# Attention with routed experts: row scaling moves from ScalarE to VectorE, narrowing and first weight splits move behind the second exponential

## The chip, the cores and the metric

The kernel runs on one NeuronCore of a Trainium2 chip. The metric is the device time of one execution in microseconds; the median of several runs counts. The engines are TensorE (PE, with its weight loads as PEld), VectorE (DVE), ScalarE (ACT), GpSimd (POOL) and SyncE (SP), which issues most of the transfers. Each engine works through its own instructions strictly in the order in which the program gives them, and waits on semaphores for the others.

## The reference

```
scores = q k^T / sqrt(D) + bias(|i - j|)         # B=2, H=8, S=576, D=64; bias by a small MLP
attn   = exp(scores - max) / (sum + 1e-9);  x = attn v        # x: N=1152 tokens x 512
expert = argmax(x w_gate); gate = softmax(x w_gate)[expert]   # E=8, at most 288 rows for one expert
moe[i] = gate[i] * relu(x[i] w1[expert]) w2[expert]           # 0 for rows over the capacity
h = moe w_in;  out = (h * cos(h)) w_out                       # 512 -> 2048 -> 512
```

A row can be multiplied by its gate before the two expert matmuls, since relu and matmuls are linear in a positive factor. This product of one tile of rows with its column of gates is the "row's scaling" of the change.

## The kernel before

The attention is cut into 36 steps (`ns`): each is one tile of 128 query rows (`BLOCKS`) and one pair of heads. `step_of(n)` is a software pipeline written out by hand: it emits, for several steps at once, what each engine is to do, and the order of emission is the order on each engine. In step n stand:

- the second exponential of step n, `emit_exp(n, 1)` (line 398, with the sum of the row read out behind it);
- the scores of step n+1 (`emit_qk`, line 381, the banks `sb` for the first head and `sa` for the second), and on VectorE the sums of score and bias with their minimum (`emit_sum`, line 389);
- the transposes of the exponentials of step n in three groups (`emit_tr`, line 412) and their copies on ScalarE (`emit_tev`, line 419, into `et`);
- in steps up to 25, the bias of later tiles: `bias_h` (line 313, four products on VectorE) and `bias_half` (line 337, matmuls into the one bank `bb`, read out on ScalarE by line 338 twice a step, so that the second half waits for the read-out of the first);
- the first exponential of step n+1, then the product with v of step n-1 (`emit_pv`, line 433, into a part of `sa`) and its copy (`emit_xs`, line 443). The next scores for `sa` wait for that copy.

When a tile of rows is complete, `finish_block` puts four small functions on a list that `run_late` works off, one or two a step: `f1` and `f2` (gate logits, line 511 on, the largest and its index; then the marks `nm`, `idxf` and `oh`, lines 523 to 526, on the engine `aux[0]`, which is GpSimd), `f3` (an exponential of 8 columns on ScalarE, line 535) and `f4` (the gate `gt`, lines 541 and 542 on VectorE, and the row's scaling, line 551 on ScalarE, which is put on the list `put_off` and emitted behind the third copy of the step). `route` (line 560) numbers the rows within their experts by matmuls with `oh` and `srun`, works out the destination of each row (`ov`, `wv`, `sl`, lines 586 to 598, on GpSimd) and scatters the rows to DRAM (line 602). For the last tile alone, behind the 36 steps, `aux[0]` is VectorE.

In steps 28 to 32 (`EARLY`) five pieces of `w_in` are narrowed to float32, each by four operations: `mag` (line 709, ScalarE), `shift`, `low` and `sign` (lines 712, 715 and 718, VectorE). `mag` stands in step n-1 ahead of `emit_xs`, that is between the two exponentials of step n. In steps 32 and 33 the first two pieces of the first expert's `w1` are split into a high and a low part (`split1`, line 908 on ScalarE, line 909 on VectorE), at the step's end, also ahead of the second exponential of the next step. In step 35 the rows of the first expert are transposed (`turned`, lines 935 to 937), and from there on the two large experts, a small one and the second layer follow, with TensorE busy nearly throughout.

Of the kernel before, what the change touches and what calls it, by code (L numbers as in the profile page):

```python
# [14 lines left out]
AF = mybir.ActivationFunctionType  # L15
ALU = mybir.AluOpType
# [7 lines left out]
DM = H * D  # L24
# [78 lines left out]
def attention_moe_kernel(  # L103
# [38 lines left out]
    eid, w_tiles = [], {}  # L142
# [350 lines left out]
    def finish_block(b, ib):  # L493
        t = tile_of(b, ib)
        loc = {}

        xs, row, rz = xs_t[b, ib], xn_t[b, ib], rz_t[b, ib]

        def f1():
            ps = late_f1()  # L500
            for p in range(NP):
                T.matmul(out=ps[32 * p:32 * p + 32, :], lhsT=wgs[:, p, :], rhs=xs[:, p, :], start=True, stop=True)
            yield
            A.activation(out=lt_buf[:, :], in_=ps[:, :], func=AF.Copy)

        def f2():
            ps = late_ps()
            T.transpose(ps, lt_buf[:, :], ident)
            yield
            lp = sm_p.tile([128, H, E], F32, tag="lp", bufs=1, name="lp")  # L510
            V.tensor_tensor(
                out=lp.rearrange("p (q u) e -> p q u e", u=2),
                in0=ps.rearrange("p (q z e) -> p q z e", q=NP, e=E)[:, :, 0:2],
                in1=rz.rearrange("p (q u) -> p q u", u=2)[:, :, :, None].to_broadcast([128, NP, 2, E]), op=ALU.mult,
            )
            lg = sm_p.tile([128, E], F32, tag="lg", name="lg")
            V.tensor_reduce(out=lg, in_=lp.rearrange("p h e -> p e h"), axis=AX.X, op=ALU.add)
            top = sm_p.tile([128, 8], F32, tag="top", bufs=2, name="top")
            V.max(out=top, in_=lg)  # L519
            ix = sm_p.tile([128, 8], U32, tag="ix", bufs=2, name="ix")  # L520
            V.max_index(out=ix, in_max=top, in_values=lg)
            nm = sm_p.tile([128, 1], F32, tag="nm", bufs=2, name="nm")
            aux[0].tensor_scalar(out=nm, in0=top[:, 0:1], scalar1=-1.0, scalar2=None, op0=ALU.mult)  # L523
            for t_, a, e in parts_of(b, t):
                aux[0].tensor_copy(idxf[a:e, t_:t_ + 1], ix[a:e, 0:1])
                aux[0].tensor_scalar(
                    out=oh[a:e, t_, :], in0=eio[a:e, 0:E], scalar1=idxf[a:e, t_:t_ + 1], scalar2=None, op0=ALU.is_equal,
                )
            loc.update(lg=lg, nm=nm)

        def f3():
            lg, nm = loc["lg"], loc["nm"]
            ex = sm_p.tile([128, E], F32, tag="ex", bufs=2, name="ex")
            es = sm_p.tile([128, 1], F32, tag="es", bufs=2, name="es")
            A.activation(out=ex, in_=lg, func=AF.Exp, bias=nm, scale=1.0, accum_out=es)
            loc["es"] = es

        def f4():
            es = loc["es"]
            gt = sm_p.tile([128, 1], F32, tag="gt", bufs=2, name="gt")  # L540
            V.tensor_scalar(out=gt, in0=es, scalar1=1e-9, scalar2=None, op0=ALU.add)
            V.reciprocal(out=gt, in_=gt)
            P.memset(row[:, DM:RW], 0.0)
            word = row[:, DM:DM + 1].bitcast(I32)
            P.iota(word, pattern=[[0, 1]], base=128 * ib if b == BOTH else b * S + 128 * ib, channel_multiplier=1)
            if b == BOTH:
                P.tensor_scalar(out=word[64:128], in0=word[64:128], scalar1=S - 64, scalar2=None, op0=ALU.add)
            if aux[0] is V:
                V.tensor_scalar(out=row[:, 0:DM], in0=row[:, 0:DM], scalar1=gt[:, 0:1], scalar2=None, op0=ALU.mult)
            else:  # L550
                put_off.append(lambda: A.activation(out=row[:, 0:DM], in_=row[:, 0:DM], func=AF.Copy, scale=gt[:, 0:1]))
            for t_, a, e in parts_of(b, t):
                row_t[t_] = row

        late.extend([(1, f1), (1, f2)] + [(0, f3)] + [(1, choose)] * ((b, ib) == CHOOSE) + [(0, f4)])
# [4 lines left out]
    def route(ts):  # L560

        def f():
            psr = late_ps()
            for i, t in enumerate(ts):
                before = [srun] + [oh[:, u, :] for u in ts[:i]]
                for j, (w, x) in enumerate([(tri, oh[:, t, :])] + [(ones, x) for x in before]):
                    T.matmul(out=psr[:, E * i:E * i + E], lhsT=w, rhs=x, start=(j == 0), stop=(j == len(before)))
            yield
            for t in ts:
                aux[0].tensor_tensor(out=srun, in0=srun, in1=oh[:, t, :], op=ALU.add)  # L570
            eng = V if len(ts) > 1 and aux[0] is V else P
# [80 lines left out]
    def first_full():  # L652
# [9 lines left out]
        V.tensor_copy(kgi, kg[0:1])  # L662
        V.tensor_scalar(out=other0, in0=gidx, scalar1=float(-E), scalar2=None, op0=ALU.add)

    def run_late(n):
        rest_ = []
        for _ in range(n):
            while late and late[0][0] <= 0:
                whole(late.pop(0)[1])
            if late:  # L670
                g = late.pop(0)[1]()
                if g:
                    next(g)
                    rest_.append(g)
        return rest_

    def go_on(rest_):
        while put_off:
            put_off.pop(0)()
        for g in rest_:  # L680
            next(g, None)

# [125 lines left out]
    def step_of(n):  # L808

        g, nxt = RUNS.get(n), RUNS.get(n + 1)  # L810
        more = None
        if n == TWICE:
            more, nxt = nxt, g + 1
        if n > 1:
            b, ib, p = steps[n - 2]
            if p == NP - 1 and n < SOONER:
                finish_block(b, ib)
                ready.append((b, ib))

        while ready and n >= ROUTE_FROM:  # L820
            tile_done(*ready.pop(0))
        if n > 0:
            emit_exp(n, 1)
        if n + 1 < ns:
            b, ib, p = steps[n + 1]
            j = BLOCKS.index((b, ib))
            for u in range(2):
                emit_qk(n + 1, u)
            if p == 0 and 0 < j < len(BLOCKS) - 1:
                fetch_q(*BLOCKS[j + 1])  # L830
            if n == 0:
                bias_h(g, on_act=ON_ACT)
        hook(n, "start")
        emit_tr(n, 0)
        hook(n, "turned")
        emit_tev(n, 0)
        if n >= LATE_FROM:
            go_on(run_late(LATE_A.get(n, 0)))
        emit_tr(n, 1)
        if n > 1:  # L840
            emit_nat(n - 2)
        emit_tev(n, 1)
        emit_tr(n, 2)
        begun = run_late(LATE_B.get(n, n < LATE_FROM))
        emit_tev(n, 2)
        while put_off:
            put_off.pop(0)()
        if nxt is not None:
            bias_h(nxt, on_act=ON_ACT if n < ACT_TO else (), quads=(0, 1))
        if n in EARLY:  # L850
            for _ in range(2):
                early_ops.pop(0)()
        go_on(begun)
        if g is not None:
            bias_half(g, 0)
        if n > 1:
            emit_nrm(n - 2)
        if n + 1 < ns:
            emit_exp(n + 1, 0)
        if nxt is not None:  # L860
            bias_h(nxt, on_act=ON_ACT if n < ACT_TO else (), quads=(2, 3))
        if n in EARLY:
            early_ops.pop(0)()
        if n + 1 in EARLY:
            early_ops.pop(0)()
        hook(n, "values")
        if 0 < n:
            emit_rz(n - 1)
            emit_pv(n - 1)
            emit_xs(n - 1)  # L870
        if n == SOONER:
            b, ib, p = steps[n - 1]
            finish_block(b, ib)
            tile_done(b, ib)
        go_on(run_late(LATE_C.get(n, 0)))
        if g is not None:
            bias_half(g, 1)
            if more is not None:
                bias_h(more, on_act=ON_ACT)
                bias_half(nxt, 0)  # L880
                bias_half(nxt, 1)
            if g == NG - 1:
                own.append(bb)
        load_step(n)
        if n in FILL_AT:
            i = FILL_AT.index(n)
            fill_rows(256 * i, min(256, E1 * CAP - 256 * i))
            if n == FILL_AT[-1]:
                fill_ids()
        if 17 <= n < 26:  # L890
            fill_out(n - 17)
        hook(n, "end")
# [81 lines left out]
    def expert_end(s, off):  # L974
# [13 lines left out]
        (28, "end"): [lambda: fetch_piece(3), lambda: fetch_w1(eid[0], (1,))],  # L988
        (29, "end"): [lambda: fetch_w1(eid[0], (2,))],
        (30, "end"): [lambda: fetch_w1(eid[0], (3,))],  # L990
        (32, "end"): [lambda: fetch_w2(eid[0], (1,)), lambda: split1(0)],
        (33, "end"): [lambda: fetch_w2(eid[0], (2,)), lambda: split1(1)],
        (34, "end"): [lambda: fetch_w2(eid[0], (3,)), part_banks],
        (35, "start"): [lambda: turned(0, (0, 1))],
        (35, "turned"): [lambda: turned(0, (2, 3))],
# [5 lines left out]
    def hook(n, at):  # L1001
        for f in hooks.get((n, at), ()):
            f()
# [18 lines left out]
    tile_done(b, ib)  # L1022
    tail = settle()
    own[0] = xb[:, 0:384]
    aux[0] = V


    st.close()
    body = ctx.enter_context(tc.tile_pool(name="body", bufs=1))
# [403 lines left out]
```

## Time and the profile before

| quantity | value |
|---|---|
| median of 3 runs | 400.34 us (400.13 to 401.8) |
| the profiled execution | 400.66 us |
| its span, first to last instruction | 398.9 us |
| mean granted TensorE clock | 0.993 of 2.4 GHz |
| attention steps | up to about 204 us |
| experts and second layer | about 200 to 398.9 us |

The span is shorter than the time by 1.76 us, which lies around it. The profiled execution is 0.32 us above the median, so a sum made against it is carried over to the median as a difference.

### The profile page before, as it was taken

To read this page: it belongs to the slowest core of one execution; us is meant where nothing else is said; L and a number is where in the kernel's file an instruction comes from. 1 tells how busy PE (TensorE), PEld (TensorE's weight loads), DVE (VectorE), ACT (ScalarE), POOL (GpSimd) and SP (SyncE) were. 2 spreads that over 40 slices of the span, in tenths; PEclk is the share of its full clock that TensorE was granted. 3 is DMA by queue.
4 is the path that set the end of the run, shared out by engine and by line. 5 is a ranking of instruction groups with operands and counts; after the bars stand their busy time and mean duration, and the time that the engine had idled before them with its cause. 6 is when DMAs were issued, how large, how long until landed. Compare 5 with 4: busy or idle time off the path is not lost. (4 is left out here: it accounts for less than half of the span.)

```text
span 398.9 us, 10628 instructions
## 1 busy us (share of the span) xinstructions
PE 367.1 (92%) x4106; PEld 284.5 (71%) x4106; DVE 290.3 (73%) x751; ACT 282.3 (71%) x641; POOL 47.9 (12%) x122
## 2 busy tenths in 40 slices
PE   7889989999999999898889979988999999999991
PEld 4345656766677676665679879945999998789871
DVE  3856667787879875697577969955778788888660
ACT  4868978888888888888864359535776666676660
POOL 2000001010101420210680202300000000000013
PEclk9999999999999999999999999999999999999997
DMA  5689765459966463989934696991031333320003
GB/s 182 178 233 260 188 182 162 133 119 255 313 166 175 145 203 112 309 227 249 328 114 140 237 150 113 361 296 54 2 106 54 105 107 106 113 100 1 2 2 130
DMA packets 47781, 63.92 MB, mean 160 GB/s; under 512 B 6757, under 2 KB 30949, under 8 KB 47722
## 3 DMA queue, kind: packets, MB, share of 16 engines
q1 hardware_dynamic: 46553, 60.67, 53.1%
q0 software_dynamic: 1168, 2.48, 1.7%
q8 instruction: 34, 0.56, 0.6%
q14 instruction: 26, 0.20, 0.2%
HBM read 41.15 MB, written 11.54 MB: 132 GB/s over the span
## 5 line engine op out<-in xcount | busy, mean ns | idle before, releaser
L313 DVE TENSOR_SCALAR h<-tt,sml 128x576 f32<-128x576 f32 x123 | 57.8, 515 | 0.7 <-PE bb L337 0.6
L398 ACT ACTIVATE e<-e,mn 128x576 f32<-128x576 f32 x72 | 55.3, 768 | 0.0
L337 PE MATMUL bb<-h,sml 128*32 128x288 f32 x448 | 39.6, 412 | 4.1 <-ACT wo L338 4.0
L419 ACT ACTIVATE et<-t 128x384 f32<-128x384 f32 x73 | 32.7, 490 | 14.2 <-PE t L412 13.0
L412 PEld LDWEIGHTS t<-ident,e 128*128 128x128 f32 x219 | 23.2, 141 | 16.1 <-issue 13.1
L338 ACT ACTIVATE wo<-bb,sml 128x288 f32<-128x288 f32 x56 | 27.9, 499 | 9.3 <-PE bb L337 7.4
L412 PE MATMUL t<-ident,e 128*128 128x128 f32 x219 | 33.0, 283 | 1.2 <-ACT e L398 0.6
L1188 PE MATMUL t<-yh,s1h 128*128 128x384 f32 (+1 forms) x88 | 27.6, 314 | 2.2 <-DVE tn L1287 1.8
L433 PE MATMUL sa<-et,wi 128*32 128x128 f32 (+1 forms) x1000 | 29.4, 262 | 0.2 <-issue 0.2
L433 PEld LDWEIGHTS sa<-et,wi 128*32 128x32 f32 x1000 | 25.6, 110 | 5.6 <-DVE mn L389 0.8
L381 PE MATMUL sa<-k,q 64*128 64x288 f32 (+1 forms) x160 | 24.5, 415 | 3.3 <-ACT wo L443 2.7
L1188 PE MATMUL t<-yl,s1h 128*128 128x384 f32 (+1 forms) x88 | 27.3, 310 | 0.1
L381 PE MATMUL sb<-k,q 64*128 64x288 f32 (+1 forms) x160 | 27.0, 449 | 0.2 <-DVE mn L389 0.2
L1188 PE MATMUL t<-yh,s1l 128*128 128x384 f32 (+1 forms) x88 | 27.1, 308 | 0.0
L389 DVE CUSTOM_DVE_ANT_0 e<-sb,keep 128x576 f32<-128x576 f32 x16 | 12.1, 756 | 19.6 <-PE sb L381 16.6
L1280 DVE TENSOR_TENSOR tn<-tn,kn 128x640 f32<-128x640 f32 (+2 forms) x18 | 13.5, 752 | 17.3 <-ACT kn L1277 17.1
L1290 ACT ACTIVATE gh<-tn 128x640 fp32r<-128x640 f32 (+2 forms) x18 | 12.0, 679 | 15.1 <-DVE tn L1287 14.8
L381 PEld LDWEIGHTS sb<-k,q 64*128 64x128 f32 (+1 forms) x160 | 10.5, 174 | 14.7 <-issue 12.6
L1253 POOL DMA_INDIRECT out_dram<-o,id x5 | 4.9, 972 | 132.1 <-ACT o L1252 130.9
L523 POOL TENSOR_SCALAR nm<-top 128x1 f32<-128x1 f32 x8 | 1.9, 234 | 156.7 <-DVE top L519 138.7
L381 PEld LDWEIGHTS sa<-k,q 64*128 64x128 f32 (+1 forms) x160 | 12.6, 175 | 10.6 <-ACT wo L443 6.7
L957 PE MATMUL hp<-xh,s1h 128*128 128x288 f32 x64 | 19.4, 303 | 0.0
(286 smaller groups left out, 1045.9 us busy)
## 6 DMA issues: line engine op xcount, KB each, us to landing
keep<-win SPq DMA_DIRECT2D x16, 512.0 KB, 4.8
keep<-wout SPq DMA_DIRECT2D x16, 512.0 KB, 3.6
w1r<-mw SPq DMA_DIRECT2D x12, 512.0 KB, 9.0
w2r<-mw SPq DMA_DIRECT2D x12, 512.0 KB, 7.8
disp<-wo SPq DMA_DIRECT2D x10, 516.0 KB, 5.2
bias<-wo SPq DMA_DIRECT2D x16, 288.0 KB, 3.5
q<-qd SPq DMA_DIRECT2D x8, 512.0 KB, 5.3
k<-kd SPq DMA_DIRECT2D x8, 288.0 KB, 6.9
```

The lines of the kernel that those rows point to most:

```text
L313: V.tensor_scalar(out=h, in0=win_, scalar1=col, scalar2=0.0, op0=ALU.add, op1=ALU.max)
L337: T.matmul(out=ps[32 * j:32 * j + 32, :], lhsT=w2s, rhs=h_t[g, j][:, c0:c0 + 288], start=True, stop=True)
L338: A.activation(out=ev_t[g][:, c0:c0 + 288], in_=ps, func=AF.Copy, scale=rst[:, g:g + 1])
L381: T.matmul(out=ps[a:e, half, 0:HS], lhsT=qt[b, ib][rows_, h, a:e], rhs=kt[c, p][rows_, u, :], start=True, stop=True)
L389: V.tensor_tensor_reduce(out=e_t[n][:, u].rearrange("p (a c) -> p a c", a=2), in0=ps[:, :, 0:288], in1=bias_of(ib, h).rearrange("p (a c) - ...
L398: A.activation(out=e_t[n][:, u], in_=e_t[n][:, u], func=AF.Exp, scale=-1.0, bias=mn_t[n][:, u:u + 1], accum_out=z_t[b, ib][:, h:h + 1],)
L412: T.transpose(ps[:, j, :], src[:, 128 * blk:128 * blk + 128], ident[:, :])
L419: A.activation(out=dst, in_=ps[:, 0:3, :], func=AF.Copy)
L433: T.matmul(out=xo[32 * i:32 * i + 32], lhsT=v_of(c, p, at_, 32), rhs=et[:, 4 if j == 4 else 5 * u + j, a:e], start=(j == 4), stop=(j == 3),)
L957: T.matmul(out=ps, lhsT=a[g % 3][:, k], rhs=x[:, k], start=(k == 0 and i == 0), stop=(k == 3 and i == 2))
L1188: T.matmul(out=sums(f, i), lhsT=w[f % 3][:, k], rhs=ya[k][x][:, o0 + a:o0 + e], start=(k == 0 and n == 0), stop=(k == 3 and n == 2),)
L1280: V.tensor_tensor(out=tn, in0=tn, in1=kn, op=ALU.subtract)
```

## The change

Four edits. The row's scaling (eight of the nine tiles; the ninth was there already) goes from ScalarE to VectorE and is emitted by the new function `made_up`, at the end of a step, or ahead of `route`'s update of `srun` where that comes sooner. `mag` goes from in front of `emit_xs` in the step before to behind the second exponential of its own step; `shift`, `low` and `sign` go together behind the second half of the step. The first two `split1` go behind the second exponential of the next step. From step 32 on, `aux[0]` is VectorE, so the last marks and destinations leave GpSimd.

```
@@ finish_block, f4
-            if aux[0] is V:
-                V.tensor_scalar(out=row[:, 0:DM], in0=row[:, 0:DM], scalar1=gt[:, 0:1], scalar2=None, op0=ALU.mult)
-            else:
-                put_off.append(lambda: A.activation(out=row[:, 0:DM], in_=row[:, 0:DM], func=AF.Copy, scale=gt[:, 0:1]))
+            put_off.append(lambda: V.tensor_scalar(out=row[:, 0:DM], in0=row[:, 0:DM], scalar1=gt[:, 0:1], scalar2=None, op0=ALU.mult))
@@ route
             yield
+            made_up()
             for t in ts:
                 aux[0].tensor_tensor(out=srun, in0=srun, in1=oh[:, t, :], op=ALU.add)
@@ (new; go_on no longer empties put_off)
+    def made_up():
+        while put_off:
+            put_off.pop(0)()
@@ step_of, behind emit_exp(n, 1) and the scores of n + 1
+        if n in EARLY:
+            early_ops.pop(0)()
+        if n == ns - 4:
+            aux[0] = V
         hook(n, "start")
...
         emit_tev(n, 2)
-        while put_off:
-            put_off.pop(0)()
         if nxt is not None:
             bias_h(nxt, on_act=ON_ACT if n < ACT_TO else (), quads=(0, 1))
-        if n in EARLY:
-            for _ in range(2):
-                early_ops.pop(0)()
         go_on(begun)
...
         if n in EARLY:
-            early_ops.pop(0)()
-        if n + 1 in EARLY:
-            early_ops.pop(0)()
+            for _ in range(3):
+                early_ops.pop(0)()
         hook(n, "values")
...
+        made_up()
         load_step(n)
@@ hooks
-        (32, "end"): [lambda: fetch_w2(eid[0], (1,)), lambda: split1(0)],
-        (33, "end"): [lambda: fetch_w2(eid[0], (2,)), lambda: split1(1)],
+        (32, "end"): [lambda: fetch_w2(eid[0], (1,))],
+        (33, "start"): [lambda: split1(0)],
+        (33, "end"): [lambda: fetch_w2(eid[0], (2,))],
+        (34, "start"): [lambda: split1(1)],
```

On ScalarE in step 7, the first with a scaling, between the third copy (`et`, line 419) and the read-out of the bias bank (`bb`, line 338), the difference is one row:

```order
 L535 ACTIVATE ex,es<-lg,nm 128x8
 L419 ACTIVATE et<-xb 128x384
-L551 ACTIVATE wo<-wo,gt 128x512
 L338 ACTIVATE wo<-bb,sml 128x288
 L398 ACTIVATE e,z<-e,mn 128x576
```

The scaling has left the queue between the copy and the read-out. On VectorE it stands at the same step's end, behind the reciprocals `rz` and ahead of the sums (line 389) of the step after next:

```order
 L452 TENSOR_SCALAR rz<-z 128x4
 L453 RECIPROCAL rz<-rz 128x4
+L548 TENSOR_SCALAR wo<-wo,gt 128x512
 L389 ISA e,mn<-sb,bias_155 128x576
 L389 ISA mn 128x1
```

The sums now come behind one more operation. On ScalarE from step 27 to the first copy of step 28, the kernel before has the scaling and `mag` (line 709) between the third copy and the copy of the product (`wo<-sa`, line 443):

```order
L419 ACTIVATE et<-xb 128x384
L551 ACTIVATE wo<-wo,gt 128x512
L398 ACTIVATE e,z<-e,mn 128x576
L709 ACTIVATE wi<-keep 128x4x128
L443 ACTIVATE wo<-sa 128x128
L398 ACTIVATE e,z<-e,mn 128x576
L419 ACTIVATE et<-t_136 128x384
```

and the changed kernel, at the same place:

```order
L419 ACTIVATE et<-xb 128x384
L398 ACTIVATE e,z<-e,mn 128x576
L443 ACTIVATE wo<-sa 128x128
L398 ACTIVATE e,z<-e,mn 128x576
L709 ACTIVATE wi<-keep 128x4x128
L419 ACTIVATE et<-t_136 128x384
```

`mag` now stands behind both exponentials and in front of the first copy. On VectorE at the end of step 33, between the gate and the sums of step 35, the changed kernel adds the scaling and what GpSimd did for two tiles (`srun`, `ov`, `wv`, `sl`; the two rows `pv` of line 579 are only moved):

```order
+L548 TENSOR_SCALAR wo<-wo,gt 128x512
+L568 TENSOR_TENSOR srun<-srun,oh 128x8 x2
+L579 ISA jk,pv<-bb,oh 128x8
+L579 ISA pv 128x1
+L579 ISA jk,pv<-bb,oh 64x8
+L579 ISA pv 64x1
+L584 TENSOR_SCALAR ov<-pv 128x1
+L584 TENSOR_SCALAR ov<-pv 64x1
+L586 TENSOR_TENSOR ov<-ov,pv 128x1
+L586 TENSOR_TENSOR ov<-ov,pv 64x1
+L589 TENSOR_SCALAR wv<-idxf,some 128x1
+L589 TENSOR_SCALAR wv<-idxf,some 64x1
```

Behind these, and still ahead of the sums, follow lines 594 and 596 for the two tiles in the same way, so that ten operations of 1 column are new there. Fifteen more (the same five lines for three tiles) are new behind the sums and the second split, ahead of the `xl` of `turned`. The order on TensorE and SyncE is unchanged.

## Rows read from the trace of the kernel before

**Rows 1.** Windows: stretch, length, then PE, PEld, DVE, ACT, POOL busy us (instructions), clock, DMA share, GB/s.
```profile
80.00:100.00 20.00, 19.65 (x313) 13.77 (x309) 15.64 (x48) 17.14 (x46) 1.41 (x5) 1.00 0.79 188
167.05:184.72 17.67, 15.99 (x244) 11.23 (x243) 15.27 (x51) 15.12 (x40) 1.22 (x5) 1.00 0.92 229
```

**Rows 2.** Timeline of PE, steps 7 and 8: start us, us, what [idle before <-releaser].
```profile
64.41 0.76 PE L381 MATMUL sb<-k,q 64*128 64x288 f32 x4
...
68.95 0.69 PE L337 MATMUL bb<-h,sml 128*32 128x288 f32 x8 [0.35 <-ACT wo L338]
69.57 0.76 PE L381 MATMUL sb<-k,q 64*128 64x288 f32 x4
...
72.50 1.28 PE L433 MATMUL sa<-et,wo 128*32 128x128 f32 x40
...
74.19 0.76 PE L381 MATMUL sb<-k,q 64*128 64x288 f32 x4
```

**Rows 3.** Timeline of PEld, step 20.
```profile
131.84 0.16 PEld L337 LDWEIGHTS bb<-h,sml 128*32 128x32 f32 x8 [0.25 <-ACT wo L338]
```

**Rows 4.** Timeline of DVE, the last tile: scaling, `srun`, and from 220.06 ten marks.
```profile
219.19 0.48 DVE L549 TENSOR_SCALAR wo<-wo,gt 128x512 f32<-128x512 f32 x1
219.59 0.35 DVE L570 TENSOR_TENSOR srun<-srun,oh 128x8 bf16<-128x8 bf16 x2
...
220.06 0.24 DVE L586 TENSOR_SCALAR ov<-pv 128x1 f32<-128x1 f32 x2
...
221.22 0.42 DVE L712 TENSOR_SCALAR wi<-wi 128x512 int32<-128x512 int32 x1
```

**Rows 5.** Timeline of DVE, the end of step 7 and the sums behind it.
```profile
69.77 0.18 DVE L453 RECIPROCAL rz<-rz 128x4 f32<-128x4 f32 x1
70.38 0.76 DVE L389 CUSTOM_DVE_ANT_0 e<-sb,bias 128x576 f32<-128x576 f32 x1 [0.43 <-PE sb L381]
...
71.74 0.94 DVE L313 TENSOR_SCALAR h<-tt,sml 128x576 f32<-128x576 f32 x2
```

**Rows 6.** Timeline of ACT, step 27.
```profile
163.89 0.72 ACT L551 ACTIVATE wo<-wo,gt 128x512 f32<-128x512 f32 x1
164.52 0.76 ACT L398 ACTIVATE e<-e,mn 128x576 f32<-128x576 f32 x1
...
165.28 0.65 ACT L709 ACTIVATE wi<-keep 128x512 f32<-128x512 f32 x1
165.83 0.25 ACT L443 ACTIVATE wo<-sa 128x128 f32<-128x128 f32 x1
```

**Rows 7.** Timeline of PE: second head's scores in step 27, transposes and product of step 34.
```profile
166.14 0.76 PE L381 MATMUL sa<-k,q 64*128 64x288 f32 x4 [1.20 <-ACT wo L443]
...
194.91 0.44 PE L412 MATMUL t<-ident,e 128*128 128x128 f32 x2 [0.55 <-ACT e L398]
...
196.23 1.30 PE L433 MATMUL sa<-et,v 128*32 128x128 f32 x40 [0.24 <-DVE mn L389]
```

**Rows 8.** Timeline of ACT, the end of step 33.
```profile
192.86 0.72 ACT L551 ACTIVATE wo<-wo,gt 128x512 f32<-128x512 f32 x1 [0.42 <-DVE gt L542]
193.48 0.61 ACT L908 ACTIVATE s1h<-w1r 128x512 fp32r<-128x512 f32 x1
194.00 0.76 ACT L398 ACTIVATE e<-e,mn 128x576 f32<-128x576 f32 x1
```

**Rows 9.** Timeline of DVE, steps 33 to 35: a split, the sums of step 35's scores, `xl`.
```profile
194.13 0.69 DVE L909 TENSOR_TENSOR s1l<-w1r,s1h 128x512 fp32r<-128x512 f32 x1 [1.07 <-ACT s1h L908]
194.74 0.75 DVE L389 CUSTOM_DVE_ANT_0 e<-sb,bias 128x576 f32<-128x576 f32 x1
...
198.96 1.20 DVE L937 TENSOR_TENSOR xl<-hp,xh 128x288 fp32r<-128x288 f32 x3 [2.32 <-ACT xh L936]
```

**Rows 10.** Timeline of POOL, ten marks of two tiles in steps 33 and 34.
```profile
193.22 0.55 POOL L586 TENSOR_SCALAR ov<-pv 128x1 f32<-128x1 f32 x2
...
195.70 0.50 POOL L598 TENSOR_SCALAR sl<-idxf,ov 128x1 int32<-128x1 f32 x2
```

**Rows 11.** Timeline of PE, the second expert's wait for its rows.
```profile
233.87 0.93 PE L935 MATMUL hp<-ident,xg 96*128 96x96 f32 x9 [2.23 <-DMA xg<-disp]
```

More of the change, by code (lines that the diff above doesn't have):

```diff
@@ L845, in step_of @@
         emit_tev(n, 2)
-        while put_off:
-            put_off.pop(0)()
         if nxt is not None:
             bias_h(nxt, on_act=ON_ACT if n < ACT_TO else (), quads=(0, 1))
-        if n in EARLY:
-            for _ in range(2):
-                early_ops.pop(0)()
         go_on(begun)
@@ L1024, in attention_moe_kernel @@
     own[0] = xb[:, 0:384]
-    aux[0] = V
     st.close()
```

## The prediction

> **What bounds the kernel now.** I first read the busy times by stretch, then PE's timeline with its waits, because PE is the engine that is busy longest and every wait of it lengthens the run unless it is given back later. In a stretch of the bias steps PE is busy 19.65 of 20.00 us, ScalarE 17.14, VectorE 15.64; in steps 28 to 31, 15.99 of 17.67, with VectorE 15.27 and ScalarE 15.12 [rows 1]. So no engine has much room, and VectorE, which gets the work, has 22% of the first stretch and 14% of the second.
>
> The timeline of PE shows what a scaling costs [rows 2]. Step 8, without one, lasts from 69.57 to 74.19, 4.62 us. Step 7, with one, lasts from 64.41 to 69.57, 5.16 us, and in it PE waits 0.35 us for ScalarE's read-out of the bias bank. The reader is to see that the read-out stands behind the scaling in ScalarE's queue, and that nobody else in that step needed the scaled row. Later, in steps 27 and 34, PE waits for the copy of the product and for the second exponential [rows 7].
>
> **Part 1, scalings in the bias steps (7, 11, 15, 20, 24).** Each is removed from ScalarE between the third copy and the read-out. The step should fall from 5.16 to 4.62: 0.54 us in steps 7, 11, 15 and 24. In step 20 only 0.25 us of wait shows, on the weight load [rows 3], and I take that. Together 4 × 0.54 + 0.25 = 2.4 us.
>
> The price is on VectorE. The row's scaling there took 0.48 us, and the next operation started 0.40 us behind its start [rows 4]. In step 7 it goes between the reciprocal that begins at 69.77 and the sums that begin at 70.38 after a wait of 0.43 for PE [rows 5]. But PE's scores come 0.54 earlier now, so that wait is no cover any more: the reciprocal ends at 69.95, the scaling at 70.43, the two sums (70.38 to 71.74, so 1.36) at 71.79. PE's product, which needs the bank that the sums read, should start at 72.50 − 0.54 = 71.96 [rows 2]. VectorE is done 0.17 us before. If this margin doesn't hold, up to 0.40 us comes back per scaling; the part then gives between 2.4 − 4 × 0.40 = 0.8 and 2.4. I take the upper end, since the rows put the sums ahead of the product, and say that the margin is thin. In the step behind, VectorE's idle fifth takes up the delay.
>
> **Part 2, step 27: scaling and `mag` leave ScalarE ahead of the copy.** The scaling holds ScalarE from 163.89 to 164.52 (0.63), `mag` from 165.28 to 165.83 (0.55) [rows 6]. PE's second head waits 1.20 us for the copy that starts at 165.83, and begins at 166.14 [rows 7]. Both operations together are 1.18, which is nearly the whole wait: the copy should come at 164.65 and the scores follow. `mag` itself goes behind the second exponential, where the first copy of the step stands behind PE's transposes; I count it at nothing there, and at up to its 0.55 if that copy is then late. The gain is 1.2 (bounds 0, if VectorE is late at once, and 1.2).
>
> **Part 3, steps 28 to 32.** Similar removals each step, but here VectorE carries the pieces of `w_in` too. The stretch of 17.67 us has 15.27 of VectorE, and one scaling (step 31) is added: 15.75. It can shrink by at most 17.67 − 15.75 = 1.9 us, at least by nothing. I take a third of it, 0.65, since VectorE's remaining gaps are behind scores and gates that no edit makes faster. So far parts 2 and 3 give 1.85.
>
> **Part 4, steps 33 and 34.** On ScalarE the second exponential of step 34 starts at 194.00, behind a wait of 0.42, the scaling (0.62) and the split (0.52) [rows 8]. All three leave, so it starts at 194.00 − 1.85 − 1.56 = 190.6, and PE's transposes lose their wait of 0.55 [rows 7]. VectorE gets more than ScalarE gives, though: scaling 0.40, `srun` and its neighbours 0.47 (219.59 to 220.06), ten marks 1.16 (220.06 to 221.22, so 0.116 each) [rows 4], all ahead of the sums of step 35. The gate that starts them is done at 192.86 − 1.85 = 191.0; 191.0 + 0.40 + 0.47 + 1.16 and about 0.2 for the reciprocals (as 69.77 to 69.95 [rows 5]) is 193.2, where the sums started at 194.74 [rows 9]. PE's product came 1.49 behind these (196.23, where it already waits 0.24 for VectorE [rows 7]), so now at 194.7. The gain of 1.85 has shrunk to 1.5.
>
> **Part 5, steps 34 and 35.** Ahead of `xl`, VectorE gets the second split, `srun` for three tiles and fifteen marks. From 193.2: two sums 1.36, the split 0.61 (194.13 to 194.74 [rows 9]), `srun` for three about 0.4 (two took 0.35 [rows 4]), fifteen marks 1.74, and two small groups that were there already, an estimated 0.5: 197.8, or 196.1 + 15 m with m for one mark. `xl` started at 198.96 and waited 2.32 for ScalarE [rows 9]; ScalarE is now some 1.5 earlier, so VectorE is the later one. The gain left is 1.1.
>
> Behind this PE is busy nearly throughout and its order does not change, so a start that is 1.1 earlier ends 1.1 earlier. The only wait of size is 2.23 us for the gathered rows of the second expert [rows 11]; I take it that the transfer moves along with the queue that issues it, whose order doesn't change either.
>
> **Sum.** 2.4 + 1.1 = 3.5 us. The profiled execution took 400.66 (span 398.9, and 1.76 around it) and the change would make it 397.2; that execution lies 0.32 above the median, so against the median of 400.34 it is 396.8 us. With part 3 at its bounds (1.25 more, 0.65 less) and part 1 at its lower one (1.6 less) it is 395.6 to 399.1. I count 0.5%, 2.0 us, as about what a measurement of this kernel can tell from no change: faster means under 398.34, slower over 402.3.
>
> **The rivals.**
>
> B: VectorE is full in the last nine steps, and parts 2 to 5 give nothing. For it: VectorE is the busier of the two there, 15.27 against 15.12 [rows 1], and work is moved to it. Against it: PE, not VectorE, names ScalarE as releaser at both ends [rows 7]. The time is 400.34 − 2.4 = 397.9.
>
> The Trainium skill bears on this ("Perfetto Trace Analysis", section "Optimizing Scalar/DVE Operations"): an operation that either engine can do is faster on DVE where a performance mode is there, but if DVE is saturated it may make sense to hand work to Scalar, the reverse of this change. The trace agrees with the first half as a duration (0.48 us against 0.72); the second half would speak for B at 397.9.
>
> C: VectorE is late in the bias steps too; the 0.17 us of margin was not there. Then four times 0.40 come back: 396.8 + 1.6 = 398.4, and with B 397.9 + 1.6 = 399.5. For it: VectorE has the whole scaling between two operations that PE waits for. Against it: 22% idle in that stretch.
>
> D: the gain is made and then lost at the gather of the second expert. If its arrival doesn't move, PE waits longer there, up to all of the 3.5: 399 to 400.5. For it: the DMAs are 79% and 92% busy in the stretches above [rows 1], so arrivals need not follow the queue. Against it: nothing in the order of transfers changes.
>
> E, the other side: marks of 1 column cost more on VectorE in the middle of the pipeline than in the quiet tail. GpSimd took (196.20 − 193.22) / 10 = 0.30 each [rows 10]. `xl` comes at 196.1 + 15 m, and the ten marks of part 4 shift its start too, by 10 (m − 0.116). With all 25 the gain of part 5 is gone at m = 0.116 + 1.1 / 25 = 0.16, and part 1's as well at 0.26. From there the kernel is slower, by 0.5% from m = 0.34, with 402.3 to 403 us. Against it: rows of this engine with the same shape say 0.116.
>
> F: more than I count. ScalarE is so far ahead after part 4 (the exponential 3.4 earlier) that PE keeps some 2.9 us there, because VectorE's marks find gaps: 400.34 − 2.4 − 2.9 = 395.0.
>
> **How the numbers follow.** The forecast, 395.6 to 397.9, has 0.50; B 0.15; C 0.10; D 0.09; E 0.05; F 0.11. The predicted time is the forecast's, 396.8. The range runs from F, 395.0, to 399.2, the upper part of C and the near end of D; outside lie half of D, E and part of F, some 0.15. Faster by over 0.5% are the forecast, F, nearly all of B and a little of C: 0.76. Within 0.5% are most of C, D and the rest of B: 0.19. Slower: 0.05.
>
> **What the profile of the changed kernel would show.** Part 1 is right if PE's waits for the bias read-out are gone and steps with a scaling last 4.62; it is wrong, and C holds, if PE's product waits there for VectorE's minimum. Nine scalings should stand on VectorE at about 0.48. Parts 2 and 3 are right if PE's waits of 1.2 for the product's copy are gone; short ones for VectorE in their place are B. For parts 4 and 5, with 2.4 from part 1, the second exponential of step 34 should start near 188.2, `xl` near 195.4, and the marks should take 0.10 to 0.12 each; at 0.26 and more E holds. The wait for the gather should stay near 2.2; if it is 4 to 6, D holds. The prediction would be most wrong if VectorE's queue in steps 27 to 35 passes its delays on from step to step, since each of my parts starts from the gain of the one before.

## The result, and the profile after

The changed kernel took 396.02 us in the median of 4 runs (395.12 to 397.51), the kernel before 400.24 in 4 runs beside it (399.38 to 401.8). The ratio is 0.9894 with a 95% interval of 0.985 to 0.9938: about 4.2 us faster, where 3.5 were forecast (396.8). The profiled execution of the changed kernel is the longest of the four, 397.51 us with a span of 395.4 and a mean granted clock of 0.989.

The steps first. Here is PE's timeline of the changed kernel in steps 7 and 8, the stretch of [rows 2].

```profile
67.93 0.67 PE L337 MATMUL bb<-h,sml 128*32 128x288 f32 x8
68.53 0.76 PE L381 MATMUL sb<-k,q 64*128 64x288 f32 x4
...
71.45 1.28 PE L433 MATMUL sa<-et,wo 128*32 128x128 f32 x40
...
73.14 0.76 PE L381 MATMUL sb<-k,q 64*128 64x288 f32 x4
```

The wait of 0.35 for the bias read-out is gone. Step 7 started at 63.92 and lasts 4.61 us like its neighbours (5.16 before). On VectorE the scaling stands between the reciprocal and the sums (the timeline that answers to [rows 5]):

```profile
69.28 0.18 DVE L453 RECIPROCAL rz<-rz 128x4 f32<-128x4 f32 x1
69.38 0.46 DVE L548 TENSOR_SCALAR wo<-wo,gt 128x512 f32<-128x512 f32 x1
69.75 0.75 DVE L389 CUSTOM_DVE_ANT_0 e<-sb,bias 128x576 f32<-128x576 f32 x1
...
71.10 0.08 DVE L389 DVE_READ_ACCUMULATOR2_ANT mn<- 128x1 f32 x1
```

VectorE no longer waits for PE's scores, and its sums are done at 71.18, shortly ahead of the product at 71.45. All nine scalings together (groups by line and shape, DVE: busy us, mean ns) are as priced:

```profile
L548 DVE TENSOR_SCALAR wo<-wo,gt 128x512 f32<-128x512 f32 x9 | 4.2, 472 | 0.1
```

From step 27 on the waits change hands. Before, PE's waits between 60 and 200 us had 2.7 us in all for the product's copy (line 443) ahead of scores. After, the list of them begins (us in total, times, longest):

```profile
PE sa L433 <- DVE mn L389: 2.9, 4, 1.3
PE hp L934 <- ACT wo L443: 0.4, 1, 0.4
```

PE now waits for VectorE's minimum, four times (0.19, 0.81, 0.55 and 1.32), and nowhere for the copy ahead of the scores. The windows tell the same. In 17 us of these steps VectorE is busy 15.98, 94%, where [rows 1] had 86% in the stretch of steps 28 to 31; in the bias steps it went from 15.64 to 16.21 of 20.

```profile
80.00:100.00 20.00, 19.84 (x315) 13.94 (x316) 16.21 (x52) 17.20 (x46) 1.39 (x5) 1.00 0.82 208
164.00:181.00 17.00, 15.45 (x251) 11.35 (x253) 15.98 (x53) 15.70 (x42) 1.38 (x8) 1.00 1.00 244
```

VectorE's timeline at the end of step 33, the place of the last block of order rows ahead of the prediction:

```profile
187.42 0.49 DVE L548 TENSOR_SCALAR wo<-wo,gt 128x512 f32<-128x512 f32 x1
...
188.29 0.22 DVE L584 TENSOR_SCALAR ov<-pv 128x1 f32<-128x1 f32 x2
...
189.43 0.74 DVE L389 CUSTOM_DVE_ANT_0 e<-sb,bias 128x576 f32<-128x576 f32 x1
...
192.25 0.27 DVE L584 TENSOR_SCALAR ov<-pv 128x1 f32<-128x1 f32 x3
...
193.77 0.28 DVE L466 TENSOR_TENSOR wo<-t,rz 128x128 f32<-128x128 f32 x1
193.97 1.18 DVE L936 TENSOR_TENSOR xl<-hp,xh 128x288 fp32r<-128x288 f32 x3
```

Ten marks take 189.43 − 188.29 = 1.14, fifteen take 193.77 − 192.25 = 1.52: 0.11 and 0.10 each. `xl` starts at 193.97 with no wait, right behind VectorE's other work, 4.99 us earlier than before; the prediction named 195.4 for it, and 188.2 for the second exponential of step 34, which starts at 186.90. PE in the same steps:

```profile
190.91 1.30 PE L433 MATMUL sa<-et,v 128*32 128x128 f32 x40 [1.32 <-DVE mn L389]
...
195.08 0.55 PE L412 MATMUL t<-ident,e 128*128 128x128 f32 x3 [0.32 <-ACT et L419]
195.39 0.38 PE L956 MATMUL hp<-xh,s1h 128*128 128x288 f32 x1
```

The first expert's matmuls, at 200.71 before, start 5.32 us earlier; 0.46 of that is a start of the whole execution that was earlier by as much (first scores of PE at 20.73, before at 21.19). The profile gained only 3.5 us of span, so some was lost behind this point. And of the 3.5, 3.15 are left in the time of the execution, since 2.11 us lie outside the span instead of 1.76: 1.96 to 2.16 us in every run whose scaling is on VectorE, 1.67 to 1.85 in every run where it is on ScalarE. No row shows what this third of a microsecond is, and the prediction carried the 1.76 over. PE's timeline and a window at the second expert show where:

```profile
226.00 0.29 PE L942 MATMUL ac<-hl,s2h 128*128 128x288 f32 x1
229.44 1.67 PE L934 MATMUL hp<-ident,xg 96*128 96x96 f32 x9 [3.15 <-DMA xg<-disp]
```

```profile
230.00:235.00 5.00, 5.00 (x33) 5.00 (x33) 4.23 (x10) 3.88 (x10) 0.00 (x0) 0.72 1.02 115
```

The wait for the rows is 3.15, where [rows 11] had 2.23: 0.92 lost in this profile (the repeat, below, has 2.83). Behind it the granted clock is 0.72 over five microseconds, and the same nine matmuls take 1.67 instead of 0.93 us; in the kernel before, the clock behind its wait stayed at 1.00. Of the 5.3 us, 4.43 are left where the rows arrive (233.87 to 229.44).

### The profile page after: what moved, and what is told of

Read it like the earlier page. It is cut to its first block, busy times and chain, and to the rows that moved or that the text cites. A ratio compares the mean times of both kernels' runs of the same rounds, so it can differ in the third digit from the quotient of the medians.

```text
span 395.4 us, 10644 instructions
## 1 busy us (share of the span) xinstructions
PE 366.4 (93%) x4106; PEld 286.0 (72%) x4106; DVE 296.8 (75%) x792; ACT 278.2 (70%) x633; POOL 38.1 (10%) x89
## 5 line engine op out<-in xcount | busy, mean ns | idle before, releaser
L1187 PEld LDWEIGHTS t<-yh,s1h 128*128 128x128 f32 x88 | 16.6, 188 | 3.6 <-DVE tn L1286 2.6
L957 ACT ACTIVATE hh<-hp 128x288 fp32r<-128x288 f32 x16 | 6.6, 410 | 17.8 <-PE hp L956 17.8
L956 PE MATMUL hp<-xl,s1h 128*128 128x288 f32 x64 | 18.9, 295 | 0.0
```

Of the source, the lines that this page charges most:

```text
L956: T.matmul(out=ps, lhsT=a[g % 3][:, k], rhs=x[:, k], start=(k == 0 and i == 0), stop=(k == 3 and i == 2))
L1187: T.matmul(out=sums(f, i), lhsT=w[f % 3][:, k], rhs=ya[k][x][:, o0 + a:o0 + e], start=(k == 0 and n == 0), stop=(k == 3 and n == 2),)
```

## The experiments

The runs that follow were made on other chips, where the kernel before took 404.17 us (the second group of runs: 404.61, the third: 400.23) and single runs scattered by 1%. So two readings are used: the ratio to the kernel before on the same chip, and the steps in the profiles, counted from PE's first scores on, since these start up to 1.45 us apart. Counted so, steps of the same order repeat within 0.15 us up to the product of step 34, with one exception: the profile of the kernel before lost 0.5 us near 187, where PE's product is in two rows, the second behind a gap that no other engine ends ([0.20 <-issue]). A later run with the same order in the steps (told near the end, with only fetches behind the steps moved) does not have it:

```profile
185.56 1.30 PE L433 MATMUL sa<-et,wi 128*32 128x128 f32 x40
...
195.57 1.30 PE L433 MATMUL sa<-et,v 128*32 128x128 f32 x40 [0.24 <-DVE mn L389]
```

That run is the base of the table, which has, in us, how much earlier than there PE comes to five places: the scores behind the last scaling of a bias step (151.75 in the base), the scores of step 30 (169.13), those of step 34 (186.79), the product that PE forms in step 34 (195.57, [rows 7]), and the first expert's matmuls (200.05).

| kernel | 151.75 | 169.13 | 186.79 | 195.57 | 200.05 | ratio to before |
|---|---|---|---|---|---|---|
| before, the profile shown ahead | −0.09 | −0.09 | −0.59 | −0.58 | −0.58 | 1 |
| changed | 2.17 | 3.49 | 4.36 | 4.28 | 4.28 | 0.9894 (0.985 to 0.9938) |
| scaling only | 2.22 | 2.61 | 2.92 | 3.63 | 2.86 | 0.9897 (0.9844 to 0.9951) |
| narrowing only | −0.01 | 0.54 | 1.82 | 1.69 | −1.60 | 0.9958 (0.9927 to 0.9989) |
| splits only | −0.07 | −0.14 | −0.12 | 0.75 | −0.15 | 0.9939 (0.9907 to 0.9971) |
| marks only | −0.05 | −0.04 | −0.01 | −0.72 | −1.13 | 0.9983 (0.995 to 1.0016) |
| changed, again | 2.18 | 3.50 | 4.37 | 4.29 | 2.11 | 0.9878 (0.9836 to 0.992) |
| changed, all marks on GpSimd | 2.16 | 3.48 | 4.35 | 5.43 | 5.43 | 0.9832 (0.9795 to 0.9869) |
| changed, destinations on GpSimd | 2.25 | 3.56 | 4.44 | 5.52 | 5.52 | 0.985 (0.9815 to 0.9886) |
| changed, scaling twice | 1.42 | 2.69 | 3.15 | 2.61 | 1.45 | one run |

In the last column profiles part that agree in the others: the changed kernel has 4.28 there and its repeat 2.11, with the same order and the same steps up to 195.57. In the repeat PE waits 1.39 us for ScalarE's copy of the product instead of 0.40, and its clock is at half behind that (told in the last section). So one profile compares two kernels up to step 34 and not behind it, and what an edit is worth in the whole is read from the ratio.

**The four edits alone.** Each was put into the kernel before by itself. The scaling alone:

```
-                put_off.append(lambda: A.activation(out=row[:, 0:DM], in_=row[:, 0:DM], func=AF.Copy, scale=gt[:, 0:1]))
+            put_off.append(lambda: V.tensor_scalar(out=row[:, 0:DM], in0=row[:, 0:DM], scalar1=gt[:, 0:1], scalar2=None, op0=ALU.mult))
...
         emit_tev(n, 2)
-        while put_off:
-            put_off.pop(0)()
...
+        made_up()
         load_step(n)
```

> The kernel before with only the row's scaling moved to VectorE. Theory A (ScalarE's queue held PE up): the bias steps give what the changed kernel showed there, about 2.3 us up to step 26, and steps 27, 31 and 33 give about 0.6 each in PE's start of the next scores: 396.2 to 397.5 in all. Rival B (VectorE full from step 27 on): only the 2.3 of the bias steps, 398.0, and waits of PE for VectorE's minimum from step 28 on.

It gives 2.22 us in the bias steps and 1.4 more by the product of step 34, 3.63 in all: theory A's places, with 0.39, 0.31 and 0.71 between them, where 0.6 each was expected. Rival B's time is out, since steps 27 to 33 gain too, though PE does wait 0.40 and 0.30 for VectorE. The waits for the product's copy shrink but stay (timeline of PE):

```profile
163.22 0.76 PE L381 MATMUL sa<-k,q 64*128 64x288 f32 x4 [0.82 <-ACT wo L443]
...
180.12 0.76 PE L381 MATMUL sa<-k,q 64*128 64x288 f32 x4 [0.47 <-ACT wo L443]
182.51 1.30 PE L433 MATMUL sa<-et,wi 128*32 128x128 f32 x40 [0.40 <-DVE mn L389]
```

By its ratio the scaling alone is worth as much as all four edits (0.9897 and 0.9894); in the steps it gives 3.63 of the 4.28.

The narrowing alone:

```
+        if n in EARLY:
+            early_ops.pop(0)()
         hook(n, "start")
...
-        if n in EARLY:
-            early_ops.pop(0)()
-        if n + 1 in EARLY:
-            early_ops.pop(0)()
+        if n in EARLY:
+            for _ in range(3):
+                early_ops.pop(0)()
         hook(n, "values")
```

> The kernel before with only the narrowing moved (mag behind the second exponential, the three VectorE pieces together). Theory A: the bias steps don't move; PE's two waits of 1.2 for the product's copy in steps 27 and 31 fall by the 0.55 of mag each, and 0.2 in step 28: 1.0 to 1.3 us, 399.0 to 399.3. Rival B: PE waits for VectorE's sums instead, 400 to 400.8.

The ratio is 0.9958, and the steps gain 1.82, half as much again as theory A had. The first wait for the copy falls from 1.20 to 0.65; the second, 1.24, is gone altogether, and PE waits 0.80 and 0.19 for VectorE at products in its place:

```profile
180.94 1.30 PE L433 MATMUL sa<-et,wi 128*32 128x128 f32 x40 [0.80 <-DVE mn L389]
```

So ScalarE's queue was the limit, and VectorE is the next one, at a lower price: B's mechanism without B's result. Behind step 34 this profile loses its gain (−1.60 at the first expert), after a wait of 2.21 for the copy of the product and with the clock at half from 198 to 204.

The splits alone, and the marks alone:

```
-        (32, "end"): [lambda: fetch_w2(eid[0], (1,)), lambda: split1(0)],
+        (32, "end"): [lambda: fetch_w2(eid[0], (1,))],
+        (33, "start"): [lambda: split1(0)],
-        (33, "end"): [lambda: fetch_w2(eid[0], (2,)), lambda: split1(1)],
+        (33, "end"): [lambda: fetch_w2(eid[0], (2,))],
+        (34, "start"): [lambda: split1(1)],
```

> The kernel before with only the first two weight splits moved behind the second exponential. Theory A: the exponential of step 34 starts 0.52 earlier and PE's wait of 0.55 there goes, 399.7 to 399.9. Rival: VectorE's half of the split comes as late as before and the sums of step 35 behind it set PE's product: no change, 400.2.

Up to the scores of step 34 nothing moves; the product in it comes 0.75 earlier, the 0.55 of theory A and the 0.24 that PE waited for VectorE there. So the rival is out for the product. But the gain is gone at the first expert (−0.15), ahead of which PE waits 0.74 and 1.06 for ScalarE (0.40 and 0.50 in the base). The ratio is more than these steps explain (0.75 us are 0.2%); its interval comes down to 0.3%, and no row was found for the rest.

```
+        if n == ns - 4:
+            aux[0] = V
         hook(n, "start")
...
     own[0] = xb[:, 0:384]
-    aux[0] = V
```

> The kernel before with only the engine of the last marks and destinations changed from GpSimd to VectorE (from step 32 on). Theory A: VectorE waits 1.07 in step 33 and 2.32 ahead of xl in step 35 in the kernel before, and the marks at 0.116 each fit mostly there; PE's wait of 0.52 for GpSimd goes: 400.0 to 400.6. Rival E (marks of one column are dear on VectorE, 0.26 us and more): xl over 2 us later, 402 or more.

The ratio shows no change, as expected, but the steps lose 0.72 at the product. PE waits 0.29 for VectorE's `oh` instead of 0.52 for GpSimd's part, and then 1.95 for VectorE's minimum:

```profile
195.90 1.30 PE L433 MATMUL sa<-et,v 128*32 128x128 f32 x40 [1.95 <-DVE mn L389]
```

So the marks did not fit in VectorE's gaps: ten of them stand ahead of its sums.

**The marks taken out of the whole.** Two versions of the changed kernel, beside the changed kernel itself. One has the first three edits alone, with `aux[0]` on GpSimd up to the end of the steps. The other moves only the five operations per tile back (`behind` is filled after the 36 steps):

```
-            eng = V if len(ts) > 1 and aux[0] is V else P
+            eng = V if len(ts) > 1 and behind else P
...
+    behind.append(1)
     spare[1] = t_bank[1]
```

> The changed kernel again, beside the three below on one chip. The steps are expected as in its first profile: the scores of step 36 of 36 start 166.2 us behind those of the first (171.3 before), and the whole is 3.5 to 5 us under the kernel before, the difference within that being PE's wait for the second expert's rows and the clock behind it.

> The changed kernel with the last marks left on GpSimd as before (its first three edits alone). By parts 4 and 5 of the prediction the 25 marks and srun cost VectorE 1.4 us ahead of the sums of step 35 and 2 us ahead of xl, all on the path: without them PE's wait of 1.3 for VectorE's minimum in step 34 is gone, PE waits 0.4 to 0.5 for GpSimd's oh instead, and the first expert's matmuls start 0.5 to 1.0 us earlier than in the changed kernel. Rival: the edit of the marks was needed, since oh and the row's destinations come late from GpSimd: the same or up to 0.8 later than the changed kernel.

> The changed kernel with nm, idxf, oh and srun on VectorE from step 32 on, but the five operations per tile that work out destinations left on GpSimd. Theory: it has both gains, no wait for oh beyond 0.3 and no marks ahead of the sums and of xl: the product of step 34 about 1.1 earlier and the first expert about 1.0 earlier than in the changed kernel. Rival: GpSimd's later scatters or the exponentials on ScalarE set the pace and it gains under 0.3.

The changed kernel's steps repeat to 0.01 us. Without the marks the product of step 34 comes 1.15 us earlier, with the destinations alone taken out 1.24. PE's timeline of the second version:

```profile
189.91 1.30 PE L433 MATMUL sa<-et,v 128*32 128x128 f32 x40 [0.15 <-DVE mn L389]
```

The wait of 1.32 is 0.15. So with the other three in, the fourth edit costs 1.15 us up to the product of step 34. What it costs the whole run is not shown: the medians agree in sign (398.53 and 398.31 against 399.53), but the intervals overlap, and these two profiles lose their lead again on the way to the second expert, where PE arrives 206.49 and 208.17 us behind the first scores (205.56 and 207.75 in the two of the changed kernel).

**VectorE's margin.** A second product of the same size behind each scaling:

```
             put_off.append(lambda: V.tensor_scalar(out=row[:, 0:DM], in0=row[:, 0:DM], scalar1=gt[:, 0:1], scalar2=None, op0=ALU.mult))
+            put_off.append(lambda: V.tensor_scalar(out=row[:, 0:DM], in0=row[:, 0:DM], scalar1=1.0, scalar2=None, op0=ALU.mult))
```

> The changed kernel with a second VectorE product of the same size (by 1.0) behind every scaling, about 0.38 us each. It weighs VectorE's margin: in step 7 of the changed kernel the sums end at 71.10 and the product of PE that needs them starts at 71.45. If the margin is near 0.35 a step with a scaling grows by 0 to 0.1 us up to step 24; if VectorE were full there (rival C) by 0.38 each, 1.9 in five steps. In steps 31 and 33, where PE already waits for VectorE's minimum (0.55 and 1.32), it should cost its full 0.38 each (rival B's mechanism).

It lost more than expected: the steps behind the scalings of steps 7, 11 and 15 grow by 0.28, 0.28 and 0.31 us, those behind steps 20 and 24 by nothing. PE's weight loads (PEld) for the product of step 8, behind the scaling of step 7, wait for VectorE:

```profile
71.64 1.03 PEld L433 LDWEIGHTS sa<-et,wo 128*32 128x32 f32 x40 [0.60 <-DVE mn L389]
```

In the changed kernel the same load starts at 71.24, 0.06 behind VectorE's minimum. So no 0.35 was left: what waits for the sums is the weight load, which is 0.21 ahead of the first matmul, and of some 0.4 that it came later the step lost 0.28. The margin is about 0.1 us. Behind the scalings of steps 31 and 33, where PE waits for VectorE anyway, 0.46 each were lost up to the product, the full price.

**The gather.** The rows of the second expert are fetched by SP behind the scatter of the last tile by GpSimd. In the changed kernel SP's queue and GpSimd's read:

```profile
216.63 1.27 POOL L600 DMA_INDIRECT disp<-wo,sl  x1 [18.88 <-DVE wi L712]
218.21 1.35 POOL L600 DMA_INDIRECT disp<-wo,sl  x1 [0.30 <-DVE hl L958]
```

```profile
218.42 0.37 SPq L167 DMA_DIRECT2D w1r<-mw  x1
219.35 0.37 SPq L172 DMA_DIRECT2D w2r<-mw  x1
224.81 0.34 SPq L153 DMA_DIRECT2D xg<-disp  x1
```

Two fetches of 512 KB go out within 1.2 us of the second scatter, and the rows are asked for 6.60 us behind it (5.58 in the kernel before, 223.55 to 229.13). By the list of SP's own waits, 4.7 us of this is waiting for the scatter to land (3.7 before). An edit of the order tests whether these fetches are the cause (part 2 of `w1` and of `w2` go behind `second_expert`, which fetches the rows):

```
-    for m, (a, c) in enumerate((((0,), (0,)), ((1,), ()), ((), (1,)), ((2,), ()), ((), (2,)), ((3,), (3,)))):
+    for m, (a, c) in enumerate((((0,), (0,)), ((1,), ()), ((), (1,)), ((), ()), ((), ()), ((2, 3), (2, 3)))):
         e0_side[m] += [second_expert] * (m == 5)
```

> The changed kernel with two 512 KB weight fetches of the second expert issued behind the fetch of its rows instead of ahead of it. If the rows come late because those fetches fill the DMA engines (over 0.8 busy from 222 to 224), PE's wait of 3.15 falls to under 2 and the end comes 1 us or more earlier. If the scatter of the last rows takes its time in any case, the wait stays within 0.4 of the changed kernel's and nothing is gained; if the weights are then late, PE waits for the split of a weight instead and it is slower.

```profile
222.79 0.34 SPq L153 DMA_DIRECT2D xg<-disp  x1
```

```profile
227.61 0.94 PE L934 MATMUL hp<-ident,xg 96*128 96x96 f32 x9 [0.22 <-DMA xg<-disp]
```

```profile
225.00:230.00 5.00, 4.78 (x40) 4.43 (x38) 3.51 (x13) 2.95 (x8) 0.00 (x0) 1.00 1.30 194
230.00:235.00 5.00, 5.00 (x40) 5.00 (x39) 4.61 (x10) 4.53 (x12) 1.31 (x1) 1.00 0.74 158
```

The second scatter began at 219.32 here, so the request comes 3.47 us behind it instead of 6.60. PE waits 0.22, the clock stays at 1.00, and the kernel takes 395.1 us beside 399.53 of the changed one: 0.9779 of the kernel before (0.9737 to 0.9822). The fetches in front were the cause of the wait: with them behind, the time from scatter to request is 3.47, 3.48 and 3.45 us in three kernels (this one and the two that follow), with them in front 4.95 to 6.60 in ten profiles. That they act by delaying the scatter's landing is what SP's wait for it says, 3.1 us here. Put into the kernel before alone:

> The kernel before with the two weight fetches behind the fetch of the second expert's rows, and nothing else changed. If the wait for the rows (2.23 there) is made by the fetches ahead of it whatever comes before, it falls under 0.5 and the kernel is 2 us or more faster, with the clock at 1.00 behind it: 0.99 or lower. If the wait only mattered because the changed kernel came to it early, the gain is under 1 us.

The wait falls from 2.23 to 0.32, as the first theory has it, but the ratio is 0.9949 (0.9918 to 0.998), 2.0 us: just the wait. The 2 us that were expected are reached, the ratio of 0.99 that was named with them is not. In the changed kernel the edit gives 4.4 us; its two profiles wait longer there (3.15 and 2.83) and have the clock at half behind the wait, which the profile of the kernel before doesn't. Both improvements together:

> The changed kernel with the destinations' five operations per tile left on GpSimd and the two weight fetches behind the rows: both gains of the runs before, 1.0 us of the first and 3 to 4 us of the second, 0.970 to 0.977 of the kernel before. If GpSimd's later scatters hold the rows up, the wait for them is back at 1 us or more and the second gain is cut by that.

394.07 us, 0.9812 of the kernel before (0.9772 to 0.9852), less than the 0.970 to 0.977 expected. No wait for the rows is left, and the second expert is reached 2.0 us earlier than with the fetches moved alone (counted from the first scores, 204.67 against 206.72). The profile doesn't keep this to its end: its clock is 0.66 in 270 to 275. Whether this version is better than the one with the fetches moved alone stays open. Both ratios are under the changed kernel's 0.9878 on the second group's chip (0.9836 to 0.992), but the interval of this one still overlaps that.

## Why the prediction was right, and where it was off

**Part 1 was right**: 2.17 us against 2.4. Steps 7, 11, 15 and 24 gave 0.55 each and step 20 gave 0.29; step 10, which has no scaling, gave 0.28 back, with a short wait of PE for ScalarE's copy (line 419) in it, which no part of the working had. The margin on VectorE that the prediction called thin (0.17) is about 0.1, and C was that close to being true.

**Part 2 was right**: 1.32 (3.49 − 2.17) against 1.2.

**Part 3 was right in size**: 0.87 (4.36 − 3.49) where 0.65 was taken between 0 and 1.9; that third of the room was a guess, so its nearness is partly luck. VectorE is busy 94%, so B's mechanism is there (PE waits 0.81 and 0.55 for VectorE's minimum), and yet the waits that it replaces were larger. By the rule of the Trainium skill weighed with B ("Perfetto Trace Analysis", section "Optimizing Scalar/DVE Operations"), a saturated VectorE may speak for giving work to Scalar; here it was nearly full, and taking work still paid, because ScalarE's queue was where PE waited.

**Part 4 was right in mechanism and price, part 5 in its price alone**: marks at 0.10 to 0.11 each (0.116 taken), VectorE the later engine, a stall at the product and a further loss up to `xl`. That further loss did not reach PE, though: in the profile shown the first expert's matmuls still have the 4.28 of the product, and PE's last wait ahead of them is 0.32 for ScalarE's copy (line 419), not for `xl`. At the product 4.28 of gain is left, where 2.4 + 1.5 = 3.9 were forecast; at `xl` 3.95 (193.97 less 20.73, against 198.30 less 21.11 in the base) where 3.5 were. That the forecast is 0.4 low there is the surplus of parts 2 to 4, less what part 1 lacked. The experiments add what the working could have said: the loss at the product is the marks' own, 1.15 us, and with GpSimd doing them PE waits only 0.56 for it in step 33, where it now waits 0.33 for VectorE.

**The step "the transfer moves along" held only in part.** The queue did move along. In both kernels the two fetches go out 0.2 and 1.1 us behind the start of the second scatter, and PE arrives 8.1 us behind it (223.55 and 231.64 before, 218.21 and 226.29 after). What did not stay is the time from there to the request for the rows, 6.60 us instead of 5.58, and so the wait is 3.15 where about 2.2 was forecast. The working had no term for what ends that time, the landing of the scatter among the fetches. That the change made it longer is not shown. With the same order of fetches it was 6.26 in the repeat of the changed kernel, 5.99, 5.26 and 5.22 in versions of it, 4.95 with the scaling alone, and 5.14 to 5.40 with one of the other three edits alone, one profile each; why it varies stays open. So D, which had 0.09 and named a wait of 4 to 6 us as its sign, is not borne out: the rows arrived 4.43 us earlier.

**The size of the sum is met with some luck.** In the profile shown the steps gave more than forecast, and the wait for the rows, the clock behind it and the time outside the span took part of it back: 400.66 − 397.51 = 3.15 us, near the 3.5 of the sum, which had none of these. The medians differ by 4.2. E is out (m was never near 0.26). F is out as well: the exponential of step 34 did come early, but PE waited 1.32 for VectorE at the product. What F had at that place, 2.4 + 2.9 = 5.3, is what the kernel with all marks on GpSimd reached, 5.43.

## What to carry to other kernels

Look for what stands ahead of a small read-out in an engine's queue and is needed by nobody soon: moving it is worth the wait that it causes, even onto the busier engine, as long as it lands between two operations with slack there. When work is moved in a bundle, test each part against the whole: three of these four edits paid alone by their ratios, and the fourth, which no ratio showed alone, cost 1.15 us of the steps with the others in. A gain upstream is only kept if what PE waits for behind it comes earlier too; where that is a transfer, ask what is queued ahead of it, and try large prefetches behind the small transfer that someone waits for.

## What the runs showed of the hardware that was not expected

Behind waits of PE, at the second expert above all, the granted clock fell to half, 1.2 of 2.4 GHz, in some profiles and not in others. In the changed kernel, by windows of one microsecond:

```profile
229.00:230.00 1.00, 0.56 (x4) 0.59 (x5) 0.00 (x0) 0.00 (x0) 0.00 (x0) 0.71 1.37 284
230.00:231.00 1.00, 1.00 (x8) 1.00 (x8) 0.36 (x1) 0.73 (x2) 0.00 (x0) 0.50 2.07 168
231.00:232.00 1.00, 1.00 (x7) 1.00 (x6) 0.95 (x3) 0.86 (x4) 0.00 (x0) 0.50 1.04 85
232.00:233.00 1.00, 1.00 (x6) 1.00 (x6) 0.92 (x3) 1.00 (x4) 0.00 (x0) 0.58 0.72 88
233.00:234.00 1.00, 1.00 (x10) 1.00 (x9) 1.00 (x3) 1.00 (x5) 0.00 (x0) 1.00 0.67 112
```

It came behind idle times of 3.15, 2.83, 2.41, 2.00 and 1.71 us, and did not behind 2.23, 2.06, 1.84 and 1.64 us in other profiles. So the length of that one wait does not decide it alone, and what does stays open. Where it happens it is a second price of a wait; how much of the scatter of the runs it makes was not worked out.

ScalarE's copy behind the product of step 34 started about 1.06 us later in some executions of the same order than in others (192.28 and 193.34 with PE's product at 190.91 and 190.98, in the changed kernel and its repeat). No row says why; this was not settled. It matters for the reading of single profiles: PE's next matmuls wait 1.39 us for it instead of 0.40. In the repeat the clock then was at 0.50 from 194 to 197, and the first expert started 2.17 us later. In the changed kernel with the fetches moved, the same wait of 1.39 had no fall of the clock behind it. PE in these two:

```profile
193.67 1.18 PE L934 MATMUL hp<-ident,xg 96*128 96x96 f32 x6 [1.39 <-ACT wo L443]
```

```profile
193.68 0.71 PE L934 MATMUL hp<-ident,xg 96*128 96x96 f32 x6 [1.39 <-ACT wo L443]
```
